# Attention and two dense layers on one core: first pair in three pieces, first weight pieces split ahead of the pair loop

## The chip, the cores and the metric

The kernel runs on one core of one Trainium2 chip. The metric is device time in microseconds of one execution, the median of several runs. The engines of the core work side by side, each through a list of its own in order: TensorE (PE, with its weight loads PEld), VectorE (DVE), ScalarE (ACT), GpSimd (POOL) and SyncE (SP), which here only issues DMAs. They wait for each other through semaphores.

## What is computed

Attention over 2 x 12 heads of 448 rows and 64 columns, with a soft cap on the scores, then two pairs of dense layers over its 896 x 768 result. All inputs of the layers arrive as 64-bit floating point.

```python
scores = (1 / sqrt(64)) * q @ k.T
scores = cap * tanh(scores / cap)
attn = exp(scores - max) ; attn = attn / (sum(attn) + 1e-9)
x = (attn @ v), heads side by side          # 896 x 768
h = x @ w_in1 ; g = where(h > 0, h, exp(min(h, 0)) - 1) ; x = g @ w_out1
h = max(x @ w_in2, 0) ; out = (h * h) @ w_out2
```

## The kernel before

**Precision.** A 32-bit value is split into a high part (rounded to the format that TensorE multiplies fast) and a low part (the rest). Each product is made of three: high x high, high x low, low x high. So each operand needs a cast (high) and a subtraction (low).

**Attention.** The 24 heads are worked as 12 pairs, n = 0 to 11; `np_` is 12. Two pairs form a group whose q, k and v are loaded together by `load_group`. For a pair, `turn` (L159) transposes k and q with TensorE into the PSUM tile `pt`: three chunks of 128 rows each and a half chunk that comes from `kz` and `qz`, padded with zeros. `high` (L178) casts `pt` on ACT into `kqh`, `low` (L186) subtracts on DVE into `kql`. `scores(n, c)` (L197) multiplies chunk c of k with all of q, c = 0 to 3, into one of two PSUM tiles `sc`. `tanh` and `exp` run on ACT into `e`; `split_p` (L227) splits `e` on DVE into `ph` and `pl`, of which there is one buffer each, in two halves i = 0, 1; `pv` (L238) multiplies them with v into the one PSUM tile `po`, and `pv_out` copies that to `pvs` on ACT. `norm` (L271) takes the row sums out by a DMA (`den`), inverts them on DVE (`rd`), writes them to memory (`far`) and reads them back spread over the partitions (`bc`). `norm_x` (L288) multiplies and splits the result into `xh`, `xl`. `pt` too has one buffer: pair n + 1 can be turned only when `low(n)` has read it.

**Order.** The program order is written by hand (`manual_schedule`): each engine works its instructions off in the order in which the code issues them. In the loop over n, pair n's tanh and exp stand beside the scores of pair n + 1, the turn of pair n + 2 and the normalisation of pairs n - 1 to n - 3.

**Weights.** `Stream` (L312) brings the weights in as pieces of 128 x 3 x 128, in the order of their use. `load` issues the DMA of the next piece into one of five buffers `wst` on SP; `open` takes the magnitude into one of three buffers `wf` (on ACT, or on DVE while `alone` is set); `clamp`, `shift`, `sign`, `low` convert the 64-bit number to 32 bit on DVE; `high` casts to `wh` and `rest` subtracts to `wl`. `start` opens pieces 0 and 1; one `advance` finishes piece i, and in it stand `clamp` and `shift` of piece i + 1, `open` of piece i + 2 and `rest` of piece i - 1. `settle` issues the last `rest`. Outside of `alone`, `low` issues the next `load`. In the kernel before, five pieces are loaded ahead of the loop, `start` and an `advance` stand at the end of pair 0, another and `settle` at the end of pair 1, so pieces 0 and 1 are split there; the others follow after the loop, where `mm_in` (L554) multiplies the first weight pieces with the x that is ready.

Of the kernel before, what the change touches and what calls it, by code (L numbers as in the profile page):

```python
# [10 lines left out]
F32 = mybir.dt.float32  # L11
F32R = mybir.dt.float32r
# [3 lines left out]
ALU = mybir.AluOpType  # L16
# [10 lines left out]
def attention_moe_kernel(  # L27
# [12 lines left out]
    nc = tc.nc  # L40
# [3 lines left out]
    P = 128  # L44
    NFULL = S // P
# [35 lines left out]
    W = 512  # L81
    nat, st = {}, {}
# [58 lines left out]
    def prep_v(n):  # L141
        if n >= len(pairs):
            return
        g, pp = divmod(n, 2)
        vh, vl = vhs[n % 2], vls[n % 2]
        for hh in range(2):
            vn = nat[g]["v"][:, 2 * pp + hh]
            h, l = (t[:, hh:NB - 1:2, :D] for t in (vh, vl))
            nc.gpsimd.tensor_copy(h, vn)
            nc.gpsimd.tensor_tensor(l, vn, h.bitcast(F32), op=ALU.subtract)  # L150
        vn = nat[g]["w"][:, pp]
        h, l = (t[:, NB - 1, :D] for t in (vh, vl))
        nc.gpsimd.tensor_copy(h, vn)
        nc.gpsimd.tensor_tensor(l, vn, h.bitcast(F32), op=ALU.subtract)
# [1 line left out]

    def turn(n):  # L159
        if n >= len(pairs):  # L160
            return
        g, pp = divmod(n, 2)
        hs = slice(2 * pp, 2 * pp + 2)
        pt = ps1.tile([P, 2, W], F32, name="pt", tag="pt")
        for u, src in enumerate("kq"):
            for c in range(NFULL):
                nc.tensor.transpose(  # L167
                    pt[:, u, c * P:(c + 1) * P],
                    nat[g][src][:, c, hs].rearrange("p h d -> p (h d)"),
                    ident,  # L170
                )
            z = kzs[g % 2][:, pp] if u == 0 else qzs[g % 2][:, hs].rearrange("p h d -> p (h d)")
            nc.tensor.transpose(pt[:, u, NFULL * P:], z, ident)
        st["pt", n] = pt

    PIECES = ((0, 1), (slice(0, 2),))

    def high(n, copy=nc.scalar.copy):  # L178
        if n >= len(pairs):
            return  # L180
        st["qk", n] = [ap_.tile([P, 2, W], F32R, name=x, tag=x) for x in ("kqh", "kql")]

        for u in PIECES[n > 0]:
            copy(st["qk", n][0][:, u], st["pt", n][:, u])

    def low(n):  # L186
        if n >= len(pairs):
            return
        h, l = st["qk", n]
        for u in PIECES[n > 0]:  # L190
            nc.vector.tensor_tensor(
                l[:, u], st["pt", n][:, u], h[:, u].bitcast(F32), op=ALU.subtract
            )
        if n % 2:
            load_group(n // 2 + 2, "kq")

    def scores(n, c):  # L197

# [241 lines left out]
    def emit(steps):  # L440
        for step in steps:
            step()
# [42 lines left out]
    with tc.manual_schedule():  # L485
# [1 line left out]
        load_group(0, "k")  # L487
        load_group(0, "q", dma=nc.scalar.dma_start)
        nc.scalar.dma_start(capt, cap.unsqueeze(0).to_broadcast([P, 1]))
        load_group(0, "v", 0)  # L490
        ws.load()
        ws.load()
        ws.load()
        fill_kq(1, nc.gpsimd)
        load_group(1, "kq")
        load_group(0, "v", 1)
        ws.load()
        ws.load()
        load_group(1, "v")
        fill_v(0, nc.gpsimd)  # L500
        fill_v(1, nc.gpsimd)
        nc.vector.reciprocal(tsc, capt)
        nc.vector.tensor_scalar(tsc, tsc, 1.0 / math.sqrt(D), None, op0=ALU.mult)
        np_ = len(pairs)
        turn(0)
        high(0)
        low(0)
        prep_v(0)
        scores(0, 0)
        scores(0, 1)  # L510
        turn(1)
        for n in range(np_):
            last = n == np_ - 1
            tanh(n, 0)
            if n:
                high(n + 1)
            tanh(n, 1)
            if not n:
                high(n + 1)
            split_p(n - 1, 1)  # L520
            exp(n, 0)
            low(n + 1)
            scores(n, 2)
            pv(n - 1, 1)
            scores(n, 3)
            turn(n + 2)
            pv_out(n - 1)
            norm(n - 2)
            tanh(n, 2)
            tanh(n, 3)  # L530
            exp(n, 1)
            prep_v(n + 1)
            emit(norm_x(n - 3, low=nc.vector))
            split_p(n, 0)
            scores(n + 1, 0)
            scores(n + 1, 1)
            pv(n, 0)
            if n % 2 == 0:
                load_group(n // 2 + 2, "v")

            if n == 0:
                emit(ws.start())
            if n < 2:
                emit(ws.advance())
            if n == 1:
                ws.settle()

        accs = itertools.count()

# [4 lines left out]
        def mm_in(s, m, acc, xh, xl, todo):  # L554
            for kc, b in todo:
                x = half(xh, kc, b), half(xl, kc, b)
                mm3(acc[:, b, :S], ws.get((s, m, kc)), x, kc == 0, kc == KC - 1)
# [8 lines left out]
        norm(np_ - 2)  # L566
        pv_out(np_ - 1)
        emit(norm_x(np_ - 3))
        while ws.done < 5:
            emit(ws.advance())  # L570
        mm_in(0, 0, begun[0], xh, xl, kb[1:7:2])
        mm_in(0, 1, begun[1], xh, xl, kb[0::2])
        norm(np_ - 1)
        emit(norm_x(np_ - 2))
        mm_in(0, 0, begun[0], xh, xl, kb[7:late_kc:2])
        mm_in(0, 1, begun[1], xh, xl, kb[1:late_kc:2])
        emit(norm_x(np_ - 1, nc.scalar.copy, nc.vector))
# [161 lines left out]
```

## Time and profile before

| | |
|---|---|
| median of 3 runs | 609.54 us (609.36 to 612.1) |
| profiled execution | 609.67 us |
| its span, first to last instruction | 607.9 us |
| PE busy | 586.5 us (96%) |
| DVE busy | 435.8 us (72%) |
| ACT busy | 334.6 us (55%) |
| POOL busy | 76.7 us (13%) |

The attention part takes about the first 130 us, the first products with weights begin at about 130 us, and from about 150 us on PE works through the dense layers. Times in rows are microseconds from the start of the span. A row of the timeline gives start, duration, engine, line, operation, what it writes and reads, how many instructions are taken together, and in brackets how long the engine was idle before and what ended that. Matmuls are pipelined: a new one starts before the one before it ends, and the durations overlap. The granted clock of PE is given as a share of its full speed of 2.4 GHz; 0.50 is 1.2 GHz. At the very start of the span the recorded clock is 1.00 while the products' own pace is the half one.

### The profile page before, as it was taken

How to read it: one execution, taken by the hardware profiler on the slowest of the kernel's cores; microseconds unless marked ns; L12 is line 12 of the kernel's file. 1: busy time of each engine (PE TensorE's matmuls, PEld its weight loads, DVE VectorE, ACT ScalarE, POOL GpSimd, SP SyncE). 2: the span in 40 equal slices, each digit the busy share in tenths (PEclk: the TensorE clock that was granted, in tenths of full speed). 3: DMA queues.
4: the chain of work that ended last, by engine and by line, in shares of the span. 5: the costliest groups of instructions: out<-in, count | busy, mean ns of one | idle time of the engine just before them, and what ended most of it. 6: DMA issues, size and time to landing. Idle time of an engine off the chain costs nothing.

```text
span 607.9 us, 8622 instructions
## 1 busy us (share of the span) xinstructions
PE 586.5 (96%) x3036; PEld 524.3 (86%) x3036; DVE 435.8 (72%) x832; ACT 334.6 (55%) x483; POOL 76.7 (13%) x102
## 2 busy tenths in 40 slices
PE   5899999898999999999999999999999999999997
PEld 3577666676999999999999999999999999999997
DVE  1899999995999888676665667666777779991000
ACT  3788988942888777643333334656666655541000
POOL 3556453400000000000000000000000012230000
PEclk9889999998999999999999999999999999999999
DMA  8734331114444333333333344333334446632000
GB/s 203 187 84 112 93 79 32 30 33 147 130 134 136 121 106 93 98 112 112 103 109 119 90 127 130 105 109 119 111 107 118 109 117 188 181 92 104 23 24 35
DMA packets 82844, 64.76 MB, mean 107 GB/s; under 512 B 38512, under 2 KB 78704, under 8 KB 82800
## 3 DMA queue, kind: packets, MB, share of 16 engines
q1 hardware_dynamic: 80800, 63.74, 36.0%
q10 hardware_dynamic: 2000, 0.46, 0.3%
q8 instruction: 24, 0.39, 0.3%
q14 instruction: 20, 0.16, 0.1%
HBM read 61.34 MB, written 2.80 MB: 106 GB/s over the span
## 4 chain that ended last, share of the span: by engine, by line
PE 86%; DVE 7%; ACT 3%; DMA 2%; issue 1%; DVEq 0%; SPq 0%; ACTq 0%
PE acc L472 19%; PE acc L473 19%; PE acc L471 19%; PE acc L670 7%; PE acc L671 6%; PE acc L669 6%; PE po L256 6%; PE sc L208 4%; DVE pl L236 3%; DVE ph L235 1%; ACT pvs L265 1%; ACT e L217 1%; PE pt L167 1%; DMA wst<-in_moe_w_in_dram 1%; DVE xn L298 1%
## 5 line engine op out<-in xcount | busy, mean ns | idle before, releaser
L471 PE MATMUL acc<-xh,wh 128*128 128x448 f32 x384 | 140.6, 366 | 2.6 <-ACT wh L414 2.3
L472 PE MATMUL acc<-xl,wh 128*128 128x448 f32 x384 | 140.4, 366 | 0.2 <-DVE xl L305 0.2
L473 PE MATMUL acc<-xh,wl 128*128 128x448 f32 x384 | 140.4, 366 | 0.0
L414 ACT CAST wh<-wf 128x384 fp32r<-128x384 f32 (+2 forms) x114 | 57.9, 508 | 100.5 <-PE acc L472 85.4
L360 ACT ACTIVATE wf<-wst 128x384 f32<-128x384 f32 (+2 forms) x130 | 70.5, 543 | 65.0 <-DVE wl L409 34.5
L409 DVE TENSOR_TENSOR wl<-wf,wh 128x384 fp32r<-128x384 f32 (+2 forms) x116 | 63.8, 550 | 55.5 <-ACT wh L414 55.3
L471 PEld LDWEIGHTS acc<-xh,wh 128*128 128x128 f32 x384 | 72.6, 189 | 9.4 <-ACT wh L414 2.9
L473 PEld LDWEIGHTS acc<-xh,wl 128*128 128x128 f32 x384 | 72.6, 189 | 5.9 <-DVE wl L409 0.6
L472 PEld LDWEIGHTS acc<-xl,wh 128*128 128x128 f32 x384 | 72.5, 189 | 5.6 <-DVE xl L305 0.5
L394 DVE SCALAR_TENSOR_TENSOR wf<-wst,wf 128x384 uint32<-128x384 uint32 (+3 forms) x132 | 71.4, 541 | 0.0
L401 DVE SCALAR_TENSOR_TENSOR wf<-wst,wf 128x384 uint32<-128x384 uint32 (+3 forms) x132 | 71.3, 540 | 0.0
L472 PE MATMUL acc<-gl,wh 128*128 128x448 f32 x192 | 70.0, 365 | 0.0
L473 PE MATMUL acc<-gh,wl 128*128 128x448 f32 x192 | 70.0, 364 | 0.0
L471 PE MATMUL acc<-gh,wh 128*128 128x448 f32 x192 | 69.8, 364 | 0.0
L409 POOL TENSOR_TENSOR late<-wf,late 128x336 fp32r<-128x336 f32 x16 | 15.2, 953 | 386.9 <-ACT late L414 386.9
L373 DVE TENSOR_SCALAR wf<-wf 128x384 uint32<-128x384 uint32 (+3 forms) x132 | 54.9, 416 | 0.6
L369 DVE TENSOR_SCALAR wf<-wf 128x384 f32<-128x384 f32 (+3 forms) x132 | 47.2, 358 | 10.0 <-ACT wf L360 10.0
L236 DVE TENSOR_TENSOR pl<-e,ph 128x1792 fp32r<-128x1792 f32 (+1 forms) x24 | 43.5, 1812 | 1.6
L217 ACT ACTIVATE e<-sc,tsc 128x896 f32<-128x896 f32 (+1 forms) x48 | 42.5, 916 | 3.3 <-PE sc L208 3.2
L656 DVE COPY o<-acc 128x432 f32<-128x432 f32 (+1 forms) x8 | 4.5, 558 | 53.8 <-PE acc L671 47.6
L670 PE MATMUL acc<-wl,gh 128*128 128x432 f32 x112 | 40.3, 359 | 0.0
L671 PE MATMUL acc<-wh,gl 128*128 128x432 f32 x112 | 40.1, 358 | 0.0
(77 smaller groups left out, 1005.5 us busy)
## 6 DMA issues: line engine op xcount, KB each, us to landing
wst<-in_moe_w_in_dram SPq DMA_DIRECT2D x64, 384.0 KB, 3.2
wst<-in_moe_w_out_dram SPq DMA_DIRECT2D x24, 384.0 KB, 3.2
wst<-in_moe_w_out_dram SPq DMA_DIRECT2D x16, 432.0 KB, 3.3
wst<-in_moe_w_out_dram SPq DMA_DIRECT2D x16, 336.0 KB, 2.9
wst<-in_moe_w_out_dram SPq DMA_DIRECT2D x12, 256.0 KB, 2.7
bc<-far SPq DMA_DIRECT2D x24, 112.0 KB, 2.8
k<-in_k_dram SPq DMA_DIRECT2D x18, 128.0 KB, 2.8
v<-in_v_dram SPq DMA_DIRECT2D x24, 96.0 KB, 2.5
```

What stands on the lines that cost most here:

```text
L236: nc.vector.tensor_tensor(l, e, h.bitcast(F32), op=ALU.subtract)
L360: nc.scalar.activation(self.f[i], hi.bitcast(F32), AF.Abs)
L373: v.tensor_scalar(fb, fb, 3, 0x3FFFFFFF, op0=ALU.logical_shift_left, op1=ALU.bitwise_and)
L394: v.scalar_tensor_tensor(out=fb, in0=hi, scalar=0xC0000000, in1=fb, op0=ALU.bitwise_and, op1=ALU.bitwise_or,)
L401: v.scalar_tensor_tensor(out=fb, in0=lo, scalar=29, in1=fb, op0=ALU.logical_shift_right, op1=ALU.bitwise_or,)
L409: (v if dst is None else nc.gpsimd).tensor_tensor(wl, self.f[i], wh.bitcast(F32), op=ALU.subtract)
L414: (v.tensor_copy if self.alone else nc.scalar.copy)(wh, self.f[i])
L471: nc.tensor.matmul(acc, w[0], x[0], start=first, stop=False)
L472: nc.tensor.matmul(acc, w[0], x[1], start=False, stop=False)
L473: nc.tensor.matmul(acc, w[1], x[0], start=False, stop=last)
L670: nc.tensor.matmul(acc, gh[:, f, gs], w[1], start=False, stop=False)
L671: nc.tensor.matmul(acc, gl[:, f, gs], w[0], start=False, stop=z)
```

## The change

- The first pair is turned in three pieces (`FIRST`): the three full chunks of k, all of q, the last half chunk of k. Behind each piece stand two idle products of the identity with itself (`warm`) and the cast of that piece on ACT, and its subtraction on DVE. Five idle products stand ahead of the first piece and three more ahead of the first scores, 14 in all; they write the tile `po` that no one reads.
- `start`, two `advance` and `settle` stand ahead of the pair loop, behind the turn of pair 1, and no longer at the ends of pairs 0 and 1.
- Of the first five weight loads two stand ahead of the v load of pair 0, and three behind the loads of group 1 (before: three and two). At the end of pair 1 two more loads are issued, pieces 5 and 6.
- Behind the loop, two pieces instead of three are split ahead of the first products; the normalisation chain of the last pair (`norm(np_ - 1)`) stands before, `settle` behind it, and one `advance` behind `norm_x(np_ - 2)`.

```diff
-    def turn(n):
+    FIRST = ((0, slice(0, NFULL)), (1, slice(0, NFULL + 1)), (0, slice(NFULL, NFULL + 1)))
+    REST = ((0, slice(0, NFULL + 1)), (1, slice(0, NFULL + 1)))
+
+    def turn(n, pieces=REST):
...
+    def first_pair():
+        warm(5)
+        cut = [(u, slice(cs.start * P, cs.stop * P)) for u, cs in FIRST]
+        st["qk", 0] = [ap_.tile([P, 2, W], F32R, name=x, tag=x) for x in ("kqh", "kql")]
+        h, l = st["qk", 0]
+        for piece, (u, cs) in zip(FIRST, cut):
+            turn(0, (piece,))
+            warm(2)
+            nc.scalar.copy(h[:, u, cs], st["pt", 0][:, u, cs])
+            if piece is not FIRST[2]:
+                nc.vector.tensor_tensor(
+                    l[:, u, cs], st["pt", 0][:, u, cs], h[:, u, cs].bitcast(F32),
+                    op=ALU.subtract,
+                )
...
+    def warm(n):
+
+        if "warm" not in st:
+            st["warm"] = ps1.tile([P, 2, W], F32, name="po", tag="po")
+        for _ in range(n):
+            nc.tensor.matmul(st["warm"][:, 0, :P], ident, ident, start=True, stop=True)
...
-        load_group(0, "v", 0)
         ws.load()
         ws.load()
-        ws.load()
+        load_group(0, "v", 0)
         fill_kq(1, nc.gpsimd)
         load_group(1, "kq")
         load_group(0, "v", 1)
-        ws.load()
-        ws.load()
+        for _ in range(3):
+            ws.load()
         load_group(1, "v")
...
-        turn(0)
-        high(0)
-        low(0)
+        first_pair()
         prep_v(0)
+        warm(3)
         scores(0, 0)
         scores(0, 1)
         turn(1)
+
+        emit(ws.start())
+        emit(ws.advance())
+        emit(ws.advance())
+        ws.settle()
         for n in range(np_):
...
-            if n == 0:
-                emit(ws.start())
-            if n < 2:
-                emit(ws.advance())
             if n == 1:
-                ws.settle()
+                ws.load()
+                ws.load()
...
-        while ws.done < 5:
+        while ws.done < 4:
             emit(ws.advance())
         mm_in(0, 0, begun[0], xh, xl, kb[1:7:2])
+        norm(np_ - 1)
+        ws.settle()
         mm_in(0, 1, begun[1], xh, xl, kb[0::2])
-        norm(np_ - 1)
         emit(norm_x(np_ - 2))
+        emit(ws.advance())
```

What this does to the lists of the engines, at three places. First DVE at the start, before the change; L191 are the low parts of pairs 0 and 1 (`kql`), L235 and L236 `split_p` of pair 0, the rows on `wf`, `wst` and `wh` steps of `Stream`:

```order
L191 TENSOR_TENSOR kql<-pt,kqh 128x512 x2
L191 TENSOR_TENSOR kql<-pt,kqh 128x1024
L235 CAST ph<-e 128x1792
L236 TENSOR_TENSOR pl<-e,ph 128x1792
L369 TENSOR_SCALAR wf<-wf 128x384
L373 TENSOR_SCALAR wf<-wf 128x384
L394 SCALAR_TENSOR_TENSOR wf<-wst,wf 128x384
L369 TENSOR_SCALAR wf<-wf 128x384
L356 TENSOR_SCALAR wf<-wst 128x384
```

The same place on DVE after the change; L379 is `open` of piece 2, then of piece 3, L190 the low parts of pair 1:

```order
L209 TENSOR_TENSOR kql<-pt,kqh 128x128
L392 TENSOR_SCALAR wf<-wf 128x384
L396 TENSOR_SCALAR wf<-wf 128x384
L417 SCALAR_TENSOR_TENSOR wf<-wst,wf 128x384
L392 TENSOR_SCALAR wf<-wf 128x384
L379 TENSOR_SCALAR wf<-wst 128x384
...
L379 TENSOR_SCALAR wf<-wst 128x384
L396 TENSOR_SCALAR wf<-wf 128x384
L424 SCALAR_TENSOR_TENSOR wf<-wst,wf 128x384
L437 CAST wh<-wf 128x384
L432 TENSOR_TENSOR wl<-wf,wh 128x384
L190 TENSOR_TENSOR kql<-pt,kqh 128x1024
```

All sixteen weight steps of pieces 0 and 1, with the two `open` of pieces 2 and 3 among them, moved from behind pair 0's and pair 1's first halves to the place between the low parts of pairs 0 and 1.

Second, the loads on SP at the start, before:

```order
L125 DMA kz_90<-in_k_dram 64x2x64 x2
L131 DMA v<-in_v_dram 128x3x64 x2
L136 DMA w<-in_v_dram 64x64 x2
L341 DMA wst<-in_moe_w_in_dram 128x3x128 x3
L116 DMA k<-in_k_dram 128x4x64 x3
...
L131 DMA v<-in_v_dram 128x3x64 x2
L136 DMA w<-in_v_dram 64x64 x2
L341 DMA wst<-in_moe_w_in_dram 128x3x128 x2
```

The same loads on SP after the change; `wst` are the weight pieces 0, 1, then 2, 3, 4:

```order
L125 DMA kz_90<-in_k_dram 64x2x64 x2
L364 DMA wst<-in_moe_w_in_dram 128x3x128 x2
L131 DMA v<-in_v_dram 128x3x64 x2
L136 DMA w<-in_v_dram 64x64 x2
L116 DMA k<-in_k_dram 128x4x64 x3
...
L131 DMA v<-in_v_dram 128x3x64 x2
L136 DMA w<-in_v_dram 64x64 x2
L364 DMA wst<-in_moe_w_in_dram 128x3x128 x3
```

Pieces 0 and 1 moved ahead of pair 0's v, and piece 2 from the early batch to the late one.

Third, DVE behind the last pair, before; L278 is `rd` of the last pair, L401 the low step of a piece, L409 `rest`:

```order
L401 SCALAR_TENSOR_TENSOR wf<-wst,wf 128x384
L394 SCALAR_TENSOR_TENSOR wf<-wst,wf 128x384
L369 TENSOR_SCALAR wf<-wf 128x384
L409 TENSOR_TENSOR wl<-wf,wh 128x384
L373 TENSOR_SCALAR wf<-wf 128x384
L401 SCALAR_TENSOR_TENSOR wf<-wst,wf 128x384
L278 RECIPROCAL rd<-den 64x14
L298 TENSOR_TENSOR xn<-pvs,bc 64x448 x2
```

The same place on DVE after the change, where L301 is `rd`, L424 the low step and L432 `rest`:

```order
L396 TENSOR_SCALAR wf<-wf 128x384
L424 SCALAR_TENSOR_TENSOR wf<-wst,wf 128x384
L301 RECIPROCAL rd<-den 64x14
L432 TENSOR_TENSOR wl<-wf,wh 128x384
L321 TENSOR_TENSOR xn<-pvs,bc 64x448 x2
L327 CAST xh<-xn 128x448
L417 SCALAR_TENSOR_TENSOR wf<-wst,wf 128x384
```

The reciprocal of the last pair moved one piece forward, ahead of `rest` of piece 3 and of the whole of piece 4.

## Rows read from the trace of the kernel before

**Rows 1.** Busy time by stretch: start:end, length, then by engine; middle of attention.
```profile
core 0: us, PE busy (x) PEld busy (x) DVE busy (x) ACT busy (x) POOL busy (x), PEclk, DMA share, GB/s
91.20:106.40 15.20, 14.54 (x82) 10.22 (x82) 14.90 (x17) 12.55 (x13) 5.36 (x8) 1.00 0.11 32
```

**Rows 2.** Timeline, weight loads on the SP queue during the first 20 us.
```profile
7.14 1.66 SPq L341 DMA_DIRECT2D wst<-in_moe_w_in_dram  x3
...
17.15 1.13 SPq L341 DMA_DIRECT2D wst<-in_moe_w_in_dram  x2
```

**Rows 3.** Landing of the first five weight loads, then of the one issued at 17.15.
```profile
DMA to landing us min/median/max: 3.6/4.0/5.0
...
DMA to landing us min/median/max: 3.8/3.8/3.8
```

**Rows 4.** Timeline, DVE in pairs 0 and 1.
```profile
15.77 1.22 DVE L191 TENSOR_TENSOR kql<-pt,kqh 128x1024 fp32r<-128x1024 f32 x1 [5.27 <-ACT kqh L184]
...
22.90 0.35 DVE L356 TENSOR_SCALAR wf<-wst 128x384 uint32<-128x384 uint32 x1
...
24.30 0.85 DVE L235 CAST ph<-e 128x1344 fp32r<-128x1344 f32 x1
...
32.57 0.68 DVE L394 SCALAR_TENSOR_TENSOR wf<-wst,wf 128x384 uint32<-128x384 uint32 x1
...
36.03 0.85 DVE L235 CAST ph<-e 128x1344 fp32r<-128x1344 f32 x1
```

**Rows 5.** Timeline, PE: turns (pt), scores (sc) and first wait for DVE.
```profile
11.09 0.57 PE L208 MATMUL sc<-kqh,kql 64*128 64x448 f32 x2
...
17.04 0.55 PE L167 MATMUL pt<-ident,k 128*128 128x128 f32 x3
...
18.69 0.37 PE L208 MATMUL sc<-kql,kqh 64*128 64x448 f32 x2
...
25.20 0.67 PE L256 MATMUL po<-ph,vh 128*128 128x448 f32 x2 [1.85 <-DVE ph L235]
...
32.38 0.74 PE L208 MATMUL sc<-kqh 64*128 64x448 f32 x2
...
40.66 0.49 PE L167 MATMUL pt<-ident,k 128*128 128x128 f32 x3
...
41.93 0.48 PE L208 MATMUL sc<-kqh 64*128 64x448 f32 x2 [0.23 <-ACT e L217]
...
51.00 0.47 PE L208 MATMUL sc<-kqh 64*128 64x448 f32 x2 [0.23 <-ACT e L217]
```

**Rows 6.** Busy time by stretch again, where the granted clock was below 1.00.
```profile
15.20:30.40 15.20, 12.59 (x62) 8.57 (x59) 12.82 (x15) 11.49 (x13) 7.98 (x11) 0.88 0.76 187
30.40:45.60 15.20, 14.97 (x85) 11.71 (x84) 13.95 (x18) 12.85 (x14) 7.96 (x8) 0.90 0.37 84
...
136.80:152.00 15.20, 12.37 (x49) 9.79 (x49) 8.70 (x21) 3.50 (x8) 1.16 (x1) 0.89 0.46 146
```

**Rows 7.** Landing times of den; timeline behind the last pair: SP, DVE, ACT, PE.
```profile
den<-pvs SPq DMA_DIRECT2D x12, 3.5 KB, 1.8
...
136.76 0.49 SPq L268 DMA_DIRECT2D den<-pvs  x1
...
137.30 1.65 SPq L341 DMA_DIRECT2D wst<-in_moe_w_in_dram  x3
...
138.36 0.55 DVE L401 SCALAR_TENSOR_TENSOR wf<-wst,wf 128x384 uint32<-128x384 uint32 x1
...
141.20 0.54 ACT L360 ACTIVATE wf<-wst 128x384 f32<-128x384 f32 x1 [3.62 <-DMA wst<-in_moe_w_in_dram]
...
142.19 0.47 PE L471 MATMUL acc<-xh,wh 128*128 128x448 f32 x1 [2.29 <-ACT wh L414]
...
143.65 0.47 SPq L280 DMA_DIRECT2D far<-rd  x1
...
149.97 0.47 PE L471 MATMUL acc<-xh,wh 128*128 128x448 f32 x1 [0.34 <-ACT xh L304]
```

More of the change, by code (lines that the diff above doesn't have):

```diff
@@ L163, in turn, with high @@
         hs = slice(2 * pp, 2 * pp + 2)
[L164 to L178, printed above, removed]
+        if ("pt", n) not in st:
+            st["pt", n] = ps1.tile([P, 2, W], F32, name="pt", tag="pt")
+        for u, cs in pieces:
+            for c in range(NFULL + 1)[cs]:
+                if c < NFULL:
+                    src = nat[g]["kq"[u]][:, c, hs].rearrange("p h d -> p (h d)")
+                elif u == 0:
+                    src = kzs[g % 2][:, pp]
+                else:
+                    src = qzs[g % 2][:, hs].rearrange("p h d -> p (h d)")
+                nc.tensor.transpose(st["pt", n][:, u, c * P:(c + 1) * P], src, ident)
+    def high(n):
         if n >= len(pairs):
@@ L181, in high @@
         st["qk", n] = [ap_.tile([P, 2, W], F32R, name=x, tag=x) for x in ("kqh", "kql")]
-        for u in PIECES[n > 0]:
-            copy(st["qk", n][0][:, u], st["pt", n][:, u])
+        nc.scalar.copy(st["qk", n][0], st["pt", n])
     def low(n):
@@ L189, in low @@
         h, l = st["qk", n]
[L190 to L193, printed above, removed]
+        nc.vector.tensor_tensor(l, st["pt", n], h.bitcast(F32), op=ALU.subtract)
         if n % 2:
             load_group(n // 2 + 2, "kq")
+    def first_pair():
[12 more added lines that the diff above has]
+                )
+        u, cs = cut[2]
+        nc.vector.tensor_tensor(
+            l[:, u, cs], st["pt", 0][:, u, cs], h[:, u, cs].bitcast(F32), op=ALU.subtract
+        )
+    def warm(n):
[3 more added lines that the diff above has]
+            nc.tensor.matmul(st["warm"][:, 0, :P], ident, ident, start=True, stop=True)
     def scores(n, c):
```

## Prediction

> **What bounds the kernel now.** I began with the table of stretches. In the middle of the attention part the tensor engine (PE) is busy 14.54 of 15.20 us and the vector engine (DVE) 14.90 [rows 1]. Both are full there, so a delay taken before it is not worked off later, and work that leaves DVE earlier is a gain only if DVE was holding PE up. From about 150 us to the end PE runs without a wait, so what counts is when it reaches the product at 149.97 [rows 7]. I then read the timeline of the first 50 us and of the stretch from 136 to 150 us, engine by engine, for what ends each wait of PE.
>
> At the start, DVE begins the low parts of pair 1 at 15.77 [rows 4], PE begins to turn pair 2 at 17.04 and begins the scores of pair 2 at 32.38, of pair 3 at 41.93, of pair 4 at 51.00 [rows 5]. So pair 1 took about 15 us, pair 2 9.55 and pair 3 9.07. Two things stretch pair 1: DVE splits weights between two halves of its own work (from about 20.8 to 24.30, and from 32.57 to 36.03 [rows 4]), for which PE waits 1.85 us at 25.20 [rows 5]; and the clock falls. Its mean is 0.88 and 0.90 in two stretches of 15.2 us [rows 6]. At half speed each missing hundredth is 2 x 0.01 x 15.2 us of slow time, so (0.12 + 0.10) x 30.4 = 6.7 us ran at 1.2 GHz, and that cost 3.3 us.
>
> At the end of attention, the load of weight piece 5 is only asked for at 137.30. ScalarE (ACT) waits 3.62 us for it at 141.20, with the cast of piece 3 queued behind on it, and PE waits 2.29 us at 142.19 [rows 7]; the clock falls again (0.89 [rows 6]: 0.11 x 30.4 = 3.3 us slow). Last, PE waits at 149.97 for the last x, whose chain starts with the DMA at 143.65 [rows 7].
>
> **Start of the program.** The three-piece split, the idle products and the earlier end of the first pair would all bring pair 0 forward. But the order of DVE now holds the whole split of weight pieces 0 and 1 ahead of the low parts of pair 1, and one step in it (`open` of piece 2) reads piece 2. The third `ws.load()` used to be issued with the first two (three from 7.14 [rows 2]). It is now behind all loads of group 1, first of the late batch. That batch began at 17.15 [rows 2]; one weight load fewer stands ahead of it, 1.66 / 3 = 0.55 us [rows 2], so piece 2 is asked for at 16.6. The load that stood there landed 3.8 us after its issue; the five early ones took 3.6 to 5.0 [rows 3]. I take 3.8, the same place in the queue: 20.4. DVE is stopped until then, with four weight steps done.
>
> The twelve steps from that `open` to the last `rest` are the same twelve that the old kernel ran in two batches: 22.90 to 24.30 and 32.57 to 36.03 [rows 4], 1.40 + 3.46 = 4.86 us: 25.3. The low parts of pair 1 take 1.22 [rows 4]: 26.5, where they ended at 17.0. PE cannot turn pair 2 before, since it writes the buffer that this step reads: it starts **9.5 us later** than 17.04 and idles some 10 us.
>
> That wait covers the other edits at the start. Without them PE would reach the turn at 17.04 at the latest; the 14 idle products have the shape of a transpose, of which three take 0.49 us at full clock [rows 5], so 2.3 us or twice that at half; even four times would fit in 9.5 us. ACT's two weight steps of 0.54 us [rows 7] ahead of pair 0's tanh fit too, and so does the v load, 1.1 us later on its queue. The second half of pair 0 was ready for DVE at 24.30 [rows 4] and is wanted only after 29.
>
> **From there to the steady state.** From a turn to the scores one pair later PE needs 51.00 - 40.66 = 10.34 us at full clock [rows 5]. After 10 us of idling I count it slow at first. The trace has two slow spells, 6.7 and 3.3 us [rows 6]; the mean, 5.0, costs 2.5 us. So the scores of pair 2 start at 26.5 + 10.3 + 2.5 = 39.3, not 32.38. Here the change gets something back: no weights are left on DVE in pairs 0 and 1. Pair 2 then takes 9.07 instead of 9.55, since its slow start is gone: pair 3 starts at 48.4 instead of 41.93. **Loss 6.5 us**, carried through the full middle.
>
> The two loads added at pair 1 cost the queue 1.1 us behind `den` of pair 0 and ahead of group 3's k and q, which are turned four pairs on: nothing.
>
> **End of attention.** Piece 5 lies in memory, so ACT's 3.62 us and PE's 2.29 us go and the clock holds. What is late next is the last x. Its reciprocal follows the low step of piece 3 on DVE (138.36 [rows 7], 0.55 long) and needs `den`, issued at 136.76 and 1.8 us under way, the median of its twelve transfers [rows 7]: about 139.0. On SP the load of piece 8 stands ahead, so `far` goes at 139.5 instead of 143.65. From `far` to the product took 149.97 - 143.65 = 6.32 us [rows 7]: 145.8. Is PE there by then? Its way to that product loses the wait of 2.29, half of the 3.3 slow microseconds and its own wait of 0.34 for x [rows 6, 7]: 149.97 - 4.28 = 145.7; so x decides, by a hair. `rest` of piece 3 now waits behind the reciprocal; done by 140.0, about when PE wants it. **Gain 4.15 us**; 4.3 if x is early and PE decides, 3.0 if the weight load beside it holds the small DMAs up by 1.2 us, as the slowest early load was against the one at 17.15 (5.0 and 3.8 [rows 3]).
>
> **Sum.** 609.67 + 6.5 - 4.15 = **612.0 us**, against the profiled execution, which stands 0.13 above the median of 609.54. Changes within 0.5% (606.5 to 612.6) are about what a measurement of this kernel can't tell from none. Bounds: landing 3.6 to 5.0 (-0.2, +1.2), slow spell 3.3 to 6.7 (-0.85, +0.85), end 3.0 to 4.3: 610.8 to 615.2.
>
> **Rivals.** (a) *DVE does not wait*: piece 2 is there when asked for. Then DVE splits in its idle time (it waited 5.27 us at 15.77 [rows 4]) and low parts and turn start as before, with neither weights nor a falling clock behind them: scores of pair 2 at 17.04 + 10.34 = 27.4 (-5.0), pair 3 9.07 later (-5.5), end -4.15: **600**. For it: a load takes at most 5.0 us [rows 3], so piece 2 would be there had it stayed with the first two. Against: the order of the queue, where piece 2 stands behind 22 other loads at about half a microsecond each. 10%.
>
> (b) *The clock holds*: the idle products bring it up and it is full at the turn; 2.5 us of slow time go: **609.5**. For it: pair 0 runs at half speed now, two products in 0.57 us at 11.09 against 0.37 at 18.69 [rows 5]. Against: it fell after much shorter idling, of which the 1.85 us at 25.20 are one part [rows 5]. The Trainium skill (TensorE: Matmul & The Clock Gate, What's actually happening) calls the throttled state the default that activity releases; by that rule too, products ahead of the idling would not help behind it. 10%.
>
> (c) *The clock comes back late*, which ends on the slower side: the refill after the idling begins with eight transposes and then scores that wait for ACT. If the slow spell exceeds 6.2 us the time passes 612.6; at 6.7 plus the turn, 2.1 us at half speed (41.93 - 40.66 less a wait of 0.23, doubled [rows 5]), it is 8.8, +1.9: **613.9**. For it: the first spell lasted 6.7 us though PE was busy in most of it [rows 6]. The same page (Part 4: PE-mode transpose) says that transposes do not count as busy for the clock as products do; the trace speaks rather against it, since between 11.09 and the full speed of 17.04, where three transposes took 0.55 us, the engine turned pair 1 [rows 5]. 14%.
>
> **How the numbers follow.** The forecast has 66%: 42 of them up to 612.6 and 24 above. Faster by over 0.5% is (a), 10%; the same 42 + 10 = 52%; slower 24 + 14 = 38%. The range leaves out (a) and the forecast's outermost landing: 609.3 to 614.5.
>
> **What would show it.** Right: DVE's `open` of piece 2 with about 9 us of idle time ended by the weight DMA; PE's first transpose of pair 2 near 26.5 with some 10 us of idle time ended by DVE; a half-speed stretch behind it; pair 3's scores near 48; no wait for ACT in the first weight products, and a short one for the last x. Wrong: that transpose near 17 (then (a)), a full clock behind the idling (b), or a last x no earlier relative to the end of pair 11, by which the time would pass 614.

## The result and the profile after

The changed kernel takes 614.4 us (median, 614.16 to 614.67) against 609.79 us for the kernel before in the same session (609.36 to 612.1): ratio 1.0065, 95% interval 1.0047 to 1.0084. It is slower by about 4.6 us. That lies above the predicted 612.0, at the upper edge of the range (609.3 to 614.5). The profiled execution took 614.31 us with a span of 612.5 (before: 609.67 and 607.9).

**Start.** Timeline of the kernel after on SP: the late batch of weight loads. Behind it, from the table of DMAs, how long that batch took to land.

```profile
15.88 1.66 SPq L364 DMA_DIRECT2D wst<-in_moe_w_in_dram  x3
```

```profile
DMA to landing us min/median/max: 3.5/4.1/5.6
```

Timeline of DVE, from the last low part of pair 0 to the low parts of pair 1, and of PE: transposes of pair 0 that wait, first scores, turn of pair 2, first scores of pairs 2 and 3.

```profile
10.29 0.29 DVE L209 TENSOR_TENSOR kql<-pt,kqh 128x128 fp32r<-128x128 f32 x1 [0.86 <-ACT kqh L202]
...
12.30 0.48 DVE L392 TENSOR_SCALAR wf<-wf 128x384 f32<-128x384 f32 x1
19.40 0.36 DVE L379 TENSOR_SCALAR wf<-wst 128x384 uint32<-128x384 uint32 x1 [6.62 <-DMA wst<-in_moe_w_in_dram]
...
24.13 1.22 DVE L190 TENSOR_TENSOR kql<-pt,kqh 128x1024 fp32r<-128x1024 f32 x1
```

```profile
7.42 0.55 PE L178 MATMUL pt<-ident,q 128*128 128x128 f32 x3 [1.27 <-DVE kql L204]
...
9.48 0.47 PE L178 MATMUL pt<-ident,kz 128*128 128x128 f32 x1 [0.73 <-DVE kql L204]
...
12.02 0.74 PE L231 MATMUL sc<-kqh 64*128 64x448 f32 x2
...
25.41 0.90 PE L178 MATMUL pt<-ident,k 128*128 128x128 f32 x3 [7.96 <-DVE kql L190]
...
36.94 0.47 PE L231 MATMUL sc<-kqh 64*128 64x448 f32 x2 [0.22 <-ACT e L240]
...
46.00 0.47 PE L231 MATMUL sc<-kqh 64*128 64x448 f32 x2 [0.23 <-ACT e L240]
```

DVE has nothing to do for 6.62 us until piece 2 is there; PE stands for 7.96 us behind it. The granted clock falls while PE still stands; the table of stretches (start:end, length, busy time of PE, PEld, DVE, ACT, POOL, granted clock, DMA share, GB/s):

```profile
15.20:30.40 15.20, 7.24 (x40) 5.50 (x39) 10.79 (x17) 7.60 (x8) 2.32 (x6) 0.78 0.75 193
```

```profile
23.00:25.00 2.00, 0.00 (x0) 0.00 (x0) 1.93 (x4) 0.00 (x0) 0.00 (x0) 0.50 0.90 202
```

The turn of pair 2 starts at 25.41 instead of 17.04, the scores of pair 3 at 46.00 instead of 41.93 [rows 5]: 4.07 us lost. The same 4.07 us are there at the end of attention: the last product of pair 11 with v stands, by the timelines of the kernel before and of the one after, at

```profile
135.42 0.37 PE L256 MATMUL po<-pl,vh 64*128 64x448 f32 x2
```

```profile
139.49 0.37 PE L279 MATMUL po<-pl,vh 64*128 64x448 f32 x2
```

**End.** Timeline of the kernel after on SP, behind it the landing time of `far` from the table of DMAs, after the change and before it, then the timeline of DVE, ACT and PE around the last x, and the table of stretches behind it.

```profile
140.83 0.49 SPq L291 DMA_DIRECT2D den<-pvs  x1
141.42 1.96 SPq L364 DMA_DIRECT2D wst<-in_moe_w_in_dram  x2
143.47 0.47 SPq L303 DMA_DIRECT2D far<-rd  x1
147.26 1.10 SPq L308 DMA_DIRECT2D bc<-far  x2
```

```profile
DMA to landing us min/median/max: 3.8/3.8/3.8
```

```profile
DMA to landing us min/median/max: 1.6/1.6/1.6
```

```profile
142.89 0.22 DVE L301 RECIPROCAL rd<-den 64x14 f32<-64x14 f32 x1
...
150.07 1.27 DVE L321 TENSOR_TENSOR xn<-pvs,bc 64x448 f32<-64x448 f32 x2 [1.79 <-DMA bc<-far]
...
151.37 0.56 ACT L327 CAST xh<-xn 128x448 fp32r<-128x448 f32 x1 [2.54 <-DVE xn L321]
...
151.99 0.74 PE L494 MATMUL acc<-xh,wh 128*128 128x448 f32 x1 [2.50 <-ACT xh L327]
```

```profile
152.00:158.00 6.00, 6.00 (x15) 5.06 (x16) 6.00 (x16) 3.06 (x6) 0.00 (x0) 0.50 0.25 73
158.00:160.00 2.00, 2.00 (x10) 1.83 (x10) 1.26 (x3) 2.00 (x4) 0.00 (x0) 0.92 0.61 198
```

The wait for piece 5 (2.29 us at 142.19 [rows 7]) is gone. But `far` stands behind two loads of 384 KB and lands 3.8 us after its issue, against 1.6 in the kernel before. The second of the two loads, issued at 143.0, itself lands 4.1 us later, at 147.1, and `far` right behind it, at 147.3. PE waits 2.50 us for the last x, where it waited 0.34 [rows 7], and then runs at half clock until about 158. From the last x to the end of the span the kernel before needs 607.9 - 149.97 = 457.9 us, the changed one 612.5 - 151.99 = 460.5. So the span's 4.6 us are +4.07 at the start, -2.05 at the end of attention (the product of the last x comes only 2.02 later, 151.99 against 149.97), and +2.6 of slow clock behind it.

### The profile page after: what moved, and what is told of

It is laid out like the page before. It is cut to its first block, busy times and chain, and to the rows that moved or that the text cites. A ratio compares the mean times of both kernels' runs of the same rounds, so it can differ in the third digit from the quotient of the medians.

```text
span 612.5 us, 8681 instructions
## 1 busy us (share of the span) xinstructions
PE 588.8 (96%) x3064; PEld 528.5 (86%) x3064; DVE 436.5 (71%) x833; ACT 335.0 (55%) x484; POOL 74.8 (12%) x102
## 4 chain that ended last, share of the span: by engine, by line
PE 84%; DVE 7%; DMA 3%; ACT 2%; issue 2%; SPq 1%; ACTq 0%; POOL 0%; DVEq 0%
PE acc L495 19%; PE acc L494 19%; PE acc L496 19%; PE acc L694 6%; PE acc L695 6%; PE acc L693 6%; PE po L279 5%; PE sc L231 3%; DVE pl L259 3%; DVE ph L258 1%; ACT pvs L288 1%; ACT e L240 1%; DVE xn L321 1%; DVE kql L190 1%; DMA q<-in_q_dram 1%
## 5 line engine op out<-in xcount | busy, mean ns | idle before, releaser
L432 DVE TENSOR_TENSOR wl<-wf,wh 128x384 fp32r<-128x384 f32 (+2 forms) x116 | 63.7, 549 | 56.9 <-ACT wh L437 56.8
L424 DVE SCALAR_TENSOR_TENSOR wf<-wst,wf 128x384 uint32<-128x384 uint32 (+3 forms) x132 | 71.2, 539 | 0.0
L432 POOL TENSOR_TENSOR late<-wf,late 128x336 fp32r<-128x336 f32 x16 | 15.2, 950 | 390.7 <-ACT late L437 390.7
```

The costliest lines, as they stand in the source:

```text
L424: v.scalar_tensor_tensor(out=fb, in0=lo, scalar=29, in1=fb, op0=ALU.logical_shift_right, op1=ALU.bitwise_or,)
L432: (v if dst is None else nc.gpsimd).tensor_tensor(wl, self.f[i], wh.bitcast(F32), op=ALU.subtract)
```

## The experiments

The table sets all kernels side by side: time, ratio to the kernel before (95% interval), and from one profiled execution each the start of PE's turn of pair 2, of pair 3's scores, of the last product of pair 11 with v, of the product of the last x, PE's wait ahead of that, and the rest of the span behind it.

| kernel | us | ratio | turn 2 | scores 3 | last v | last x | wait | rest |
|---|---|---|---|---|---|---|---|---|
| before | 609.79 | 1 | 17.04 | 41.93 | 135.42 | 149.97 | 0.34 | 457.9 |
| after | 614.4 | 1.0065 (1.0047-1.0084) | 25.41 | 46.00 | 139.49 | 151.99 | 2.50 | 460.5 |
| e1 four early | 609.47 | 0.9964 (0.9946-0.9982) | 19.70 | 40.40 | 135.15 | 147.66 | 2.51 | 460.5 |
| e2 small first | 611.5 | 1.0011 (0.9997-1.0025) | 25.75 | 46.67 | 140.40 | 151.30 | 0.90 | 457.9 |
| e3 end only | 609.42 | 0.9972 (0.9957-0.9987) | 16.80 | 42.19 | 135.25 | 147.43 | 2.19 | 459.2 |
| e4 no idle products | 614.43 | 1.0049 (1.0034-1.0065) | 25.90 | 47.24 | 140.81 | 153.16 | 2.35 | 459.4 |
| e5 idle products at the end | 613.0 | 1.0048 (1.0031-1.0064) | 25.65 | 46.44 | 139.99 | 153.23 | 0.99 | 457.9 |
| e6 both repairs | 606.84 | 0.9942 (0.9924-0.9960) | 19.79 | 41.46 | 135.82 | 146.88 | 1.05 | 457.9 |
| e7 both, plain first pair | 605.1 | 0.9919 (0.9904-0.9934) | 19.51 | 41.08 | 134.77 | 145.42 | 0.62 | 457.9 |
| e8 end and small first | 605.76 | 0.9933 (0.9918-0.9947) | 16.97 | 42.35 | 135.41 | 146.12 | 0.70 | 457.9 |
| e9 idle products in the wait | 613.26 | 1.0051 (1.0024-1.0078) | 25.82 | 45.00 | 138.50 | 150.90 | 2.39 | 460.6 |
| e10 first pair alone | 611.91 | 1.0016 (0.9998-1.0034) | 18.11 | 42.71 | 136.32 | 151.55 | 1.20 | 457.9 |
| e11 one early, then pair 0 | 604.85 | 0.9919 (0.9892-0.9946) | 16.37 | 39.39 | 134.47 | 145.10 | 0.63 | 457.9 |
| e12 one early, then pair 1 | 604.29 | 0.9902 (0.9885-0.9920) | 17.78 | 39.12 | 133.76 | 144.39 | 0.63 | 457.9 |

The kernel before had medians of 610.56, 610.02 and 610.78 beside e1 to e4, e5 to e8 and e9 to e12; the ratios take that into account. The changed kernel's time stands beside the 609.79. Between kernels of different sessions a difference of times is uncertain by about 1 us; the other columns are read from one execution each.

**e1: is the wait for piece 2 the loss?**

```diff
-        ws.load()
-        ws.load()
+        for _ in range(4):
+            ws.load()
         load_group(0, "v", 0)
...
-        for _ in range(3):
-            ws.load()
+        ws.load()
         load_group(1, "v")
```

> The changed kernel with one edit: weight pieces 0 to 3 are all asked for ahead of pair 0's v, only piece 4 late. Theory W: the early loss is VectorE's wait for piece 2 (6.62 us at 19.40), with pair 1's low parts queued behind it. Then the step that opens piece 2 finds it there, the sixteen weight steps run from about 10.8 to 17.5, pair 1's low parts start near 17.5 instead of 24.13, pair 2's turn near 18.7 instead of 25.41, without a slow spell behind it, pair 3's scores near 38.5 instead of 46.0: 607 us (605.5 to 608.5), faster than both kernels. Rival S: the sixteen steps in front of pair 1, or the three-piece first pair, cost the time themselves, whatever the loads: pair 3's scores stay behind 44 and the time above 612.

In the timeline of e1 DVE opens piece 2 without a wait, PE waits 2.46 us instead of 7.96, and pair 3's scores stand at 40.40:

```profile
12.58 0.35 DVE L379 TENSOR_SCALAR wf<-wst 128x384 uint32<-128x384 uint32 x1
...
18.43 1.22 DVE L190 TENSOR_TENSOR kql<-pt,kqh 128x1024 fp32r<-128x1024 f32 x1
```

```profile
19.70 0.55 PE L178 MATMUL pt<-ident,k 128*128 128x128 f32 x3 [2.46 <-DVE kql L190]
...
40.40 0.47 PE L231 MATMUL sc<-kqh 64*128 64x448 f32 x2 [0.22 <-ACT e L240]
```

The mechanism holds: 4.9 us come back by the times, 4.3 by the column of the last x. Of the expected 7.4 two parts are missing. First, pair 3's scores stand at 40.40 and not at 38.5: the turn comes 1.0 us later than expected, and the clock still falls behind PE's wait of 2.46 us (0.89 in 15.2 to 30.4). Second, pair 3 starts 1.53 us earlier than in the kernel before, but the last product with v only 0.27. The lead is still 1.57 us at the scores of pair 4 (49.43 against 51.00) and 0.34 at those of pair 5 (59.74 against 60.08). In between stands DVE's first normalisation, where DVE waits for `bc`. Its chain starts on SP with `den` at 41.25, 0.85 us behind pair 3's scores, while in the kernel before it goes 0.94 us ahead of them (40.99): SP is still busy with loads, one behind the other, among them the two that the change adds at pair 1. Timeline of SP and of DVE in e1:

```profile
34.07 1.06 SPq L364 DMA_DIRECT2D wst<-in_moe_w_in_dram  x2
...
41.25 0.55 SPq L291 DMA_DIRECT2D den<-pvs  x1
```

```profile
46.94 0.62 DVE L321 TENSOR_TENSOR xn<-pvs,bc 64x448 f32<-64x448 f32 x1 [0.69 <-DMA bc<-far]
48.72 0.74 DVE L321 TENSOR_TENSOR xn<-pvs,bc 64x448 f32<-64x448 f32 x1 [1.16 <-DMA bc<-far]
```

The slow clock behind the last x stays in the profiled execution (rest 460.5). Probably not in every run: of the eight the two with a mean clock of 0.996 and 0.997 took 607.03 and 607.1, the six with 0.991 to 0.994 took 608.8 to 610.0; a mean doesn't say where in the span the clock was low.

**e2: do the large loads hold up the last x?**

```diff
+        ws.hold = True
         while ws.done < 4:
             emit(ws.advance())
         mm_in(0, 0, begun[0], xh, xl, kb[1:7:2])
         norm(np_ - 1)
+        ws.hold = False
+        ws.load()
+        ws.load()
```

While `hold` is set, `low` issues no load; the cut leaves out that condition in `Stream`.

> The changed kernel with one edit: the two weight loads that VectorE's steps for pieces 2 and 3 ask for at the end of attention are issued behind the last pair's small DMAs (far, bc) and not ahead of them. Theory D: far took 3.8 us instead of 1.6 because two weight loads of 384 KB stood just ahead of it, so the last x came late, TensorE idled 2.50 us at 151.99 and its clock was at half for some 6 us behind. Then far lands 1.6 to 1.9 after its issue, the product with the last x comes with a wait of at most 0.4 us, the clock stays full: 609.4 us (608.7 to 610.2). Rival: the chain is late by itself (reciprocal, broadcast): far stays above 3 us and the time within 1 us of 614.4.

Timeline of SP in e2, the landing time of its `far`, the product of the last x on PE, and the stretch from 136.8 to 152 (clock 1.00):

```profile
144.06 0.46 SPq L303 DMA_DIRECT2D far<-rd  x1
145.73 2.03 SPq L308 DMA_DIRECT2D bc<-far  x2
```

```profile
DMA to landing us min/median/max: 1.6/1.6/1.6
```

```profile
151.30 0.47 PE L495 MATMUL acc<-xh,wh 128*128 128x448 f32 x1 [0.90 <-ACT xh L327]
```

```profile
136.80:152.00 15.20, 14.12 (x69) 11.44 (x67) 12.75 (x25) 4.46 (x8) 2.82 (x2) 1.00 0.26 79
```

`far` lands 1.6 us after its issue again, the wait falls to 0.90 and the clock holds: 2.9 us less than the changed kernel. Expected were 5.0 less; the start was 0.67 us later than there by pair 3 and 0.91 by pair 11, and the wait is 0.90 instead of 0.4 at most. So the mechanism is shown and its price was set too high.

**e3: the end of the change alone**, on the kernel before (pieces 5 and 6 loaded at pair 1, two pieces split behind the loop, `norm(np_ - 1)` early).

```diff
             if n == 1:
                 ws.settle()
+                ws.load()
+                ws.load()
...
-        while ws.done < 5:
+        while ws.done < 4:
             emit(ws.advance())
         mm_in(0, 0, begun[0], xh, xl, kb[1:7:2])
+        norm(np_ - 1)
+        ws.settle()
         mm_in(0, 1, begun[1], xh, xl, kb[0::2])
-        norm(np_ - 1)
         emit(norm_x(np_ - 2))
+        emit(ws.advance())
```

> The kernel before with the end of the change alone: two more loads at pair 1, two pieces instead of three ahead of the first products, the last pair's normalisation and settle moved forward. Theory D: the load of piece 5 is no longer waited for, but far is held up by the weight loads ahead of it, so the product with the last x comes 2.0 us earlier than before and the slow clock behind its wait costs 2.6: 610.3 us (609.3 to 611), no gain. Rival (the prediction's term): the end part is worth 4.15 us: 605.6.

It gains 1.1 us by the medians (1.7 by the ratio) of the 4.15 predicted for it: the last x comes 2.54 us earlier (147.43), with `far` landing 3.5 us after its issue, and 1.3 us of that are given back to the clock. The three of its ten runs with a mean clock of 0.996 or 0.997 took 607.15 to 607.67.

**e4: the change without its idle products.**

```diff
-        warm(5)
...
-            warm(2)
...
-        warm(3)
```

> The changed kernel without the 14 idle products. Theory W: all that lies ahead of piece 2's landing is covered by VectorE's wait, so the first scores start about 1.3 us earlier (10.7 instead of 12.02) and nothing else moves: 614.4 us (613.7 to 615.1). Rival I: the idle products pay by the clock; without them pair 2's turn comes later or slower and the time passes 615.5.

The time is the expected one, 614.43 against 614.4. The trace says that this is partly chance: the loads of piece 2 go out 0.4 us later and the slow spell behind the turn is longer (mean clock 0.68 in 15.2 to 30.4 against 0.78), so pair 3's scores and the last x come 1.2 us later; the slow stretch at the end costs 1.1 us less in this execution (459.4 against 460.5). So the idle products bring about a microsecond by pair 3 at best, which no time resolves.

**e5: is the slow clock at the end owed to the wait for x?** The same kernel as the changed one, with ten idle products put into that wait.

```diff
         emit(norm_x(np_ - 1, nc.scalar.copy, nc.vector))
+        del st["warm"]
+        warm(10)
```

> The changed kernel with ten idle products more on the tensor engine, between its last product of weights 0 and 1 (149.1) and the products of the last x (151.99), where it stood idle for 2.50 us. Ten products of two instructions, 0.21 us each at half clock, are some 2.1 us at full clock, so they fit in the wait. Theory C (the second slow spell is owed to that idling): the clock stays full behind 152, the 16 or so products that ran at half speed (152.0 to 158.2, 2.6 us of cost) run at full speed, and the time falls from 614.3 to 611.8 (611.3 to 612.5); the last x comes no earlier. Rival P (the spell is owed to something else in that stretch, such as the low share of products before it): the clock falls as before, 614.3 (613.8 to 614.8).

Timeline of PE in e5, then the stretch in which the changed kernel's clock was 0.60, and a row of DVE:

```profile
149.24 2.39 PE L218 MATMUL po<-ident 128*128 128x128 f32 x20
...
153.23 0.47 PE L494 MATMUL acc<-xh,wh 128*128 128x448 f32 x1 [0.99 <-ACT xh L327]
```

```profile
152.00:160.00 8.00, 6.83 (x33) 5.88 (x32) 7.37 (x18) 4.39 (x8) 0.00 (x0) 1.00 0.29 85
```

```profile
151.96 0.62 DVE L321 TENSOR_TENSOR xn<-pvs,bc 64x448 f32<-64x448 f32 x1 [0.66 <-DMA bc<-far]
```

The clock holds, and the rest of the span is 457.9 us, as in the kernel before. So the 2.6 us are the price of the clock. The time falls by 1.4 us only, since the last x came 1.24 later in this run; 0.5 of that it had behind it at pair 11 already (139.99 against 139.49). The other 0.7 is a wait of DVE of 0.66 us for the second `bc`; in the changed kernel both were there at 150.07.

**e6 to e8: both repairs, and what the start is worth.** e6 takes e1 and e2 together. e7 is e6 with the first pair turned, cast and lowered whole (not in halves, as its expectation says) and without idle products. e8 is e3 with the order on SP of e2, so with the start of the kernel before. For e7:

```diff
-        first_pair()
+        turn(0)
+        high(0)
+        low(0)
         prep_v(0)
-        warm(3)
```

> The changed kernel with both repairs: four weight loads ahead of group 1's loads, and at the end the small transfers of the last x issued ahead of the large weight loads. Theory: the two losses are separate and add up. Four early loads alone came out at 609.5; the small transfers first took 2.9 us off the changed kernel, its wait for the last x fell from 2.5 to 0.9 us and the slow clock behind it went. So 609.5 - 2.9 = 606.6 (605.8 to 607.4): no wait of DVE for piece 2, pair 3's scores near 40.4, wait for the last x under 1 us, clock 1.00 from 136.8 on. Rival: the two are not separate (the pieces that are now late again behind the small transfers, or a full queue, bring the wait to the first products of weights), 608 or more.

> As the kernel with both repairs, but with the first pair as in the kernel before: turned whole, cast and lowered in halves, and no idle products at the start. It tells what the three pieces and the idle products are worth once DVE no longer waits for piece 2. Theory D: they cost, since the pieces take turns with DVE's low parts and the first scores come at 12.0 instead of 9.2; DVE starts on the weights about 0.5 us earlier (10.5 instead of 11.0) and everything behind moves with it: 0.5 us less than with both repairs, 606.1 (605.5 to 606.6). Rival I: without idle products the clock is lower in the first 30 us; 1 to 2 us more than with both repairs, 608. Third: within 0.3 us of it, since the turn of pair 2 waits for DVE either way.

> The kernel before with the end of the change and with the small transfers of the last x ahead of the weight loads; the start is that of the kernel before. Theory: the end part alone gave 609.4 with a wait for x of 2.2 us and 3 us at half speed behind it. With the small transfers first the wait falls to about 0.9 (-1.3) and the slow stretch goes (-1.3): 606.8 (606.2 to 607.5), clock 1.00 from 136.8 on. Compared with the kernel with both repairs it tells what the whole start of the change is worth: by the trace of four early loads, whose pair 3 scores stood at 40.4 against 41.9, the start should be worth 1.5 us, so this one should be slower than both repairs by about that. Rival: the start is worth nothing, both the same within 0.4 us.

The repairs add up: 606.84. The repaired end alone gives 605.76, less than expected, so it is the better part of the change. The start of the change brings nothing on top of it: e6, which has it, was expected 1.5 us faster than e8 and is 1.1 us slower by the medians, 0.76 by the last x; the single runs of the two overlap, so that the time alone doesn't tell whether it costs. Two parts of that start work against each other. The three pieces and their idle products cost 1.7 us there (e7 against e6; expected was 0.5), 1.46 of them by the last x: 0.4 at pair 3, 1.05 at pair 11, the rest in the wait for x. The early loads and weight steps gain: e7, which has all of them and the plain first pair, is 0.7 us faster than e8 by the medians and by the last x. What joins between pairs 3 and 11 is a wait of DVE for `bc` in the first normalisation, which e7 doesn't have; timeline of DVE in e6:

```profile
49.10 0.62 DVE L321 TENSOR_TENSOR xn<-pvs,bc 64x448 f32<-64x448 f32 x1 [1.09 <-DMA bc<-far]
```

**e9: the slow spell at the start.** Thirty idle products while PE waits for DVE.

```diff
+            if not n:
+                warm(30)
             turn(n + 2)
```

> The changed kernel with thirty idle products on the tensor engine while it waits for DVE ahead of the turn of pair 2 (some 8 us; thirty products of two instructions are 6.3 us at full clock). It prices the slow spell of the start by itself. Theory C (the spell follows the idling): the turn of pair 2 stays at 25.4, runs at full clock, and the 3.2 us at half speed that followed it go: 1.6 us less, 612.7 (612.2 to 613.3). Rival: the spell comes anyway, since the turn begins with transposes and waits for ScalarE follow: 614.3 (613.8 to 614.8).

The stretch from 15.2 to 30.4 of e9, then its timeline on PE:

```profile
15.20:30.40 15.20, 13.51 (x105) 12.11 (x104) 10.38 (x17) 9.03 (x10) 2.32 (x6) 1.00 0.77 196
```

```profile
25.82 0.55 PE L178 MATMUL pt<-ident,k 128*128 128x128 f32 x3 [1.69 <-DVE kql L190]
...
45.00 0.47 PE L231 MATMUL sc<-kqh 64*128 64x448 f32 x2 [0.21 <-ACT e L240]
```

The clock is 1.00 where it was 0.78, and from the turn to pair 3's scores PE takes 19.18 us instead of 20.59: the spell costs 1.4 us. In the ratio 0.9 us show, which the scatter of these runs (611.65 to 617.28) doesn't settle; the trace does.

**e10: the first pair alone**, all else as in the kernel before.

```diff
-        turn(0)
-        high(0)
-        low(0)
+        first_pair()
         prep_v(0)
+        warm(3)
```

> The kernel before with the first pair of the change alone: three pieces and idle products; all loads, the weight steps and the end as before. It prices that edit where no wait of DVE for piece 2 covers it. Theory D (the pieces serialize with DVE's low parts and delay the program): first scores near 12.0 instead of 9.2, turn of pair 1 0.8 to 1.8 us later than 12.7, and the low parts of pair 1, which DVE waits for here, as much later: 1.2 us over the kernel before, 611 (610.4 to 611.8). Rival I: the idle products keep the clock up in the first 30 us and pay that back: 609.8 (609.3 to 610.3) or less.

Timeline of e10: first scores (9.23 in the kernel before), then DVE's low parts of pair 1 (15.77 there [rows 4]):

```profile
12.69 0.74 PE L231 MATMUL sc<-kqh 64*128 64x448 f32 x2
```

```profile
16.83 1.23 DVE L190 TENSOR_TENSOR kql<-pt,kqh 128x1024 fp32r<-128x1024 f32 x1 [5.58 <-ACT kqh L184]
```

Both are later, by 3.46 and 1.06 us, and at pair 11 0.9 us are left. The time, 1.0016 with an interval of 0.9998 to 1.0034, agrees with that but doesn't resolve it by itself.

**e11 and e12: only one batch of weight steps early.** As e7, but only the first `advance` stands ahead of the loop; the second at the end of pair 0 (e11) or of pair 1 (e12). The cut is that of e12; e11 has `n == 0` in it.

```diff
         emit(ws.start())
         emit(ws.advance())
-        emit(ws.advance())
-        ws.settle()
         for n in range(np_):
...
+            if n == 1:
+                emit(ws.advance())
+                ws.settle()
```

> Both repairs and the plain first pair, but only the first batch of eight weight steps on DVE ahead of the low parts of pair 1, in the 5 us in which DVE would idle there; the second batch behind pair 0's second half, as in the kernel before. Theory F (only the batch that fits into DVE's idle time is free): the turn of pair 2 starts near 17 instead of 19.5; PE still waits some 2 us near 25 for the second batch; pair 3's scores near 40.9, 604.8 (604.0 to 605.6), at or a little under the 605.1 with both batches early. Rival: the work of DVE up to pair 3 is the same, and so is the time: 605.1 within 0.3; then DVE is full there whatever the order.

> The same with the second batch one pair later, behind pair 1's second half, the second place it has in the kernel before. Theory F: the wait of 2 us near 25 goes too and about 1 us comes back near 36: pair 3's scores near 40.4, 604.3 (603.5 to 605.2). Rival: as in the run with the second batch behind pair 0, 605.1 within 0.3.

e12 is the fastest, 604.29 us, 0.9902 (0.9885 to 0.9920) of the kernel before; its last x comes 1.03 us earlier than in e7. The time of e11 lies where its theory and its rival meet (604.8, and 605.1 within 0.3) and doesn't separate them. Timeline of DVE in e12: the low parts of pair 1 still wait for ACT, so the eight early steps fit into time that DVE had to spare; later DVE waits for the first `bc`. PE no longer waits 3.20 us for the low parts, as in e7, and the mean granted clock of e12's profiled execution is 1.000 (e7: 0.994), so part of its gain may be the clock; no run separates the two.

```profile
16.50 1.23 DVE L190 TENSOR_TENSOR kql<-pt,kqh 128x1024 fp32r<-128x1024 f32 x1 [1.71 <-ACT kqh L184]
...
46.36 1.70 DVE L321 TENSOR_TENSOR xn<-pvs,bc 64x448 f32<-64x448 f32 x2 [1.54 <-DMA bc<-far]
```

By pair 3 e11 and e12 are 2.54 and 2.81 us ahead of the kernel before, at pair 11 0.95 and 1.66. That wait for `bc`, 2.36 us in e11, is what a faster start meets next. Earlier `den`, `far` and `bc` on SP were not tried.

## Why the prediction was right or wrong

**The sign and the first mechanism were right.** DVE stops for piece 2, PE behind it, the clock falls, and the loss goes through the full middle unchanged (4.07 at pair 3, 4.07 at pair 11). e1 takes the wait away and 4.9 us come back. That the time still lies in the forecast's range, 0.1 us from its edge, is in part luck: two terms at the end were 4.7 us too favourable, and the loss at the start was 2.4 too large.

**The loss was sized too large, 6.5 for 4.07.** Piece 2 was asked for at 15.88, not 16.6, and landed 3.5 us later, not 3.8: 1.0 us. The load that no longer stands ahead was priced well: from the first early weight load to the next load SP took 1.70 us before (7.14 to 8.84) and 1.12 after (4.75 to 5.87), 0.58 less where 0.55 was predicted. Most of the rest of the 1.27 us lies in other loads, such as the two `kz` of group 1 (1.67 us before, 1.29 after); why these were shorter stays open. The twelve steps took 4.73 us (4.86 predicted). The slow spell was the other miss: I took 5.0 us at half clock, 2.5 lost; the turn of pair 2 to the scores took 36.94 - 25.41 = 11.53 us instead of 10.34, so 1.2 were lost, and e9 gives 1.4 with pair 3. The 5.0 came from mean granted clocks, and such a mean counts idle time too. Here it would make 0.22 x 30.4 = 6.7 us at half speed, but the clock was at 0.50 while PE still stood (23.0 to 25.0), and products ran slow only from 25.41 to about 28.6, some 3.2 us.

**The end was sized too large, 4.15 for 2.05.** `far` went out as predicted: 143.47, less the 4.07 of the start 139.4, against 139.5. The step that failed is the 6.32 us from `far` to the product, which took 8.52 (143.47 to 151.99). That number came from a queue on which the last large load had gone out some 5 us before `far`. The bound for that, 1.2 us, was drawn from loads among loads; measured were 2.2 (3.8 against 1.6). The Trainium skill (DMA: Bandwidth & Descriptors, Queues, rings and completion order) says that a transfer's completion lands only after every earlier write of the same DMA engine; the trace agrees, with the load ahead of `far` landing at 147.1 and `far` at 147.3. e2, which takes the loads out of its way, shows 1.6 again.

**"The clock holds" was wrong.** I let it hold at the end because the wait for piece 5 goes; a wait of 2.50 us for x took its place, and the clock fell behind it: 2.6 us that stand nowhere in the sum. e5 shows it alone. So the time passes 614, which the prediction named as the sign of a last x that comes no earlier behind pair 11; it does come 2.05 us earlier, and the clock takes that back. This term and the last one, 2.1 + 2.6, less the 2.4 by which the loss was too large, make the 2.3 us between the forecast and the result.

**The rivals.** (a), DVE does not wait, did not come; but e1 shows that its price was wrong too: without the wait the start gains 0.27 us at pair 11, not 5.5, because DVE's own work and then `bc` hold pair 3 and what follows. The loss ahead of the full stretch was carried through whole; of a lead 0.27 of 1.53 us was left in e1, and 1.66 of 2.81 in e12. (b), a full clock at the turn, fell: the first three transposes of the turn took 0.90 us, where e9 at full clock shows 0.55. (c), a clock late to return, fell too, though by its own measure, the mean clock, the spell was 6.7 us and longer than the 6.2 it asked for: only 3.2 us of it had products in it, and it cost 1.2 to 1.4 us, not more than the 2.5 assumed. Its time, 613.9, is near the result, but by another spell, at the other end.

**What hid the other edits** was the wait for DVE, as the prediction said: the three pieces and the idle products bring the first scores to 12.02 instead of 9.2 (10.50 without the idle products, in e4), and that shows in no time until the wait is gone (1.7 us between e6 and e7). The 14 idle products, priced at 2.3 us at full clock and 4.6 at half, took 6.3 (2.50, 0.61, 0.84 and 2.34); each is two instructions in the trace, where a transpose is one. The prediction counted the pieces as bringing pair 0 forward, which was wrong: PE's next piece waits for DVE to finish reading the tile `pt` (1.27 and 0.73 us in the rows above). All three pieces stand in that one tile; no run gave them tiles of their own, so that this is the reason isn't shown.

## What to carry to other kernels

A small transfer on the critical chain should be issued ahead of large loads on its queue (here that was worth 2.2 us of landing time), and a price for it holds only for the queue it was read from. A wait that is removed is worth less than its length when another as long takes its place: the clock can fall behind that one as well, so each wait left over must be looked at for its length and for the clock behind it. Give an engine early work only up to the time it has to spare there: by the last x, all of the weight steps early (e7) were worth 0.7 us against none early (e8), and half of them early (e12) 1.7.

## What the runs showed of the hardware

- `far`, 3.5 KB, landed 1.6 us after its issue with the queue free (before, e2) and 3.5 to 3.8 us with two loads of 384 KB just ahead of it (after, e1, e3, e4, e5, e9).
- The granted clock fell to half behind the waits of 2.19 to 2.51 us for the last x (after, e1, e3, e4, e9) and stayed full behind those of 0.34 to 1.20 us. The length of a wait alone doesn't decide: at 25 us, with waits of 1.85 and 0.52 us, it fell in the kernel before (0.75 in 22.8 to 30.4), and with 1.97 and 0.52 it held in e8 (1.00). How much a fall behind the last x cost differed too: 2.6 us in the profile of e1, 1.3 in that of e3. Idle products in the gap kept the clock full in e5 (1.00 where it was 0.60) and, at the start, in e9 (1.00 where it was 0.78). The Trainium skill (TensorE: Matmul & The Clock Gate, What's actually happening) calls the slow state the default that activity releases; these runs agree.
- An idle product of 128 x 128 in 32-bit floating point is two instructions in the trace (`x10` for five): ten instructions took 2.50 us at the start of the program, sixty 6.86 us in e9 at full clock.
